# Row tiles in the third block of the first layer, sums of that block in A, and a new spread of the last copies

## The chip, the cores and the metric

One core of a Trainium2 chip runs the whole program in one launch. The metric is the device time of that launch in microseconds (us), the median over runs; less is better.

## The reference

An mLSTM attention over 2 x 8 heads and 768 steps gives 1536 tokens of 320 numbers. Two dense layers follow, each with a hidden width of 2048:

```python
def _moe_ref(x, w_in, w_out):          # the first layer
    h = x @ w_in
    g = where(h >= 1, h, where(h <= -1, 0.0, (h + 1) ** 2 / 4))
    return g @ w_out

def _moe2_ref(x, w_in, w_out):         # the second layer
    h = x @ w_in
    g = maximum(h, 0.0) + log1p(exp(-abs(h)))
    return g @ w_out
```

All is float32. Every product is made of two-part numbers, a high part and a rest, so that three matmuls (high x high, rest x high, high x rest) stand for one.

## The kernel before, in words

The tokens are cut into three blocks of 512 (`BLOCKS`, j = 0, 1, 2), the hidden width into 16 strips of 128 (f). PE takes, for every layer l and block j, an **up** step per strip (h = x times w_in, in PSUM) and a **down** step (g times w_out, summed over the strips in PSUM). Between them ACT and DVE make g: in the first layer `hinge` (ACT relu L834, ACT square L839, DVE min/max L843, which reads h again), in the second `softplus` (ACT L853, DVE L857, ACT L862, DVE L866); `split_g` then makes the high part gh (ACT L875) and the rest gl (DVE L879).

PSUM has eight banks here: one each for `ha` and `hb` (the h of even and odd strips), three in the tile D (`banks[1]`, key `ACC`) and three in the tile A (`banks[0]`, key `MIX`).

* The first layer works on the full 128-row array. `up` (L760 to L770) is 8 matmuls of 512 columns for a strip; `down1` (L885 to L902, matmuls L895 to L901) is 8 more, all of them into D. A block's sums leave D through `to_x` (L904 to L935): ACT and DVE copy them to the high part xh and the rest xl of the next layer's input, and the next block's sums wait for that.
* The second layer works on two **row tiles** of 64 rows, which take two matmuls at the same time. `slot` (L779 to L787) issues such a pair; every matmul of it has the line L783. `up2` (L800 to L827) does two strips f and f+1 in 8 slots and then 7 slots, 15 in all, since the last partial product needs only 64 rows; in the second half the row tiles swap banks. Two row tiles must not sum into one bank at the same time, so where a bank changes tiles, `hand_over` (L774 to L778) puts a no-op on POOL that waits for the matmuls that come first, and the matmul that comes next waits for POOL. `down2` (L941 on) does two strips in 24 slots of 320 columns, of which 3 are put between the halves of a later up pair.

What goes out in which order is set by `Plan` (L37 on), a list scheduler that knows each task's engine, cost, what it reads and writes, and for PE tasks a place `at`. Its result is a fixed order for each engine; the hardware waits only on semaphores. The second half of an up pair carries the key `("turn", ...)`, which the 3 down slots write, so that they come between. In the loop at the end, the first layer's `down1` comes `LAG = 3` strips after its `up`; the second layer's `down2` starts only with its own strips, so the first two up pairs of the second layer have nothing between their halves.

The last block's sums lie in A bank 2 and D banks 2, 0 and 1; four copies (L995 on DVE, L997 on ACT) bring them to SBUF and eight DMAs (L1008, on SP's, ACT's and POOL's queues) write them out.

Of the kernel before, what the change touches and what calls it, by code (L numbers as in the profile page):

```python
# [22 lines left out]
DM = H * D  # L23
# [186 lines left out]
def mlstm_moe_moe(ctx: ExitStack, tc: tile.TileContext, gates, late, qk, tok, ident, w1, w2, out):  # L210
    nc = tc.nc

    def pool(name, bufs, stack=ctx, **kw):
        return stack.enter_context(tc.tile_pool(name=name, bufs=bufs, **kw))

    BUFS = dict(raw=2, v=2, w=NF, u=3, gh=4, gl=4, xr=1, qx=3, tok=2, f=3, dec=2, sig=2, vi=2, ve=2,
                den=2, y=1, v2=10, e=3, o=4, x2=1, ha=1, hb=1, D=1, A=1)
    pools, tiles = {}, {}
# [34 lines left out]
    def vec(c):  # L253
        return 0.065 + c / 960
# [7 lines left out]
    def act(c):  # L262
        return 0.09 + c / 1075
# [494 lines left out]
    def up(l, j, f, at):  # L758
# [41 lines left out]
    def up2(j, f, at):  # L800
        n = BLOCKS[j][1]
        W, HP = ([(k, 1) + x for x in ((f,), (f + 1,))] if k == "w" else [(k, 1, j, f), (k, 1, j, f + 1)] for k in "wh")
        turn = {}

        def parts(i, r, s, e):
            w, hp = tiles[W[i]], tiles[HP[i]]
            ops = [(w[:, a + 128 * k:a + 128 * k + 128], xs) for k in range(2)
                   for a, xs in ((0, xh[j][:, k]), (0, xl[j][:, k]), (WC, xh[j][:, k]))]
            ops.append((w[:, 256:384], xh[j][:, 2]))
            if i == r:  # L810
                ops.append((w[:, WC + 256:WC + 384], tiles["x2", j] if r else xh[j][:, 2]))
# [8 lines left out]
        rd = [(W[i], k) for i in range(2) for k in range(2)] + xkeys(j) + [(("x2", j % 2),)]  # L820
        add("pe", 8 * (n / 2400 + 0.013), t, reads=rd, writes=[(x,) for x in HP],
            new=[(("ha", "hb")[i], HP[i]) for i in range(2)], at=at)

        def t():
            for k, pair in enumerate(zip(parts(1, 0, False, True), parts(0, 1, False, True))):
                slot(pair, None if k else turn.pop(0))
        add("pe", 7 * (n / 2400 + 0.013), t, reads=[*rd, (("turn", at - 40),)], writes=[(x,) for x in HP], at=at + 2)  # L827

    def hinge(j, f):
        n = BLOCKS[j][1]  # L830
        HP, U = ("h", 0, j, f), ("u", 0, j, f)
# [13 lines left out]
        add("dve", vec(n), t, reads=[(HP,)], writes=[(U,)])  # L845
        return U
# [23 lines left out]
    def split_g(l, j, f, G):  # L870
        n = BLOCKS[j][1]
        GH, GL = ("gh", l, j, f), ("gl", l, j, f)

        def t():
            nc.scalar.copy(new("gh", GH, [128, n], F32R), tiles[G])  # L875
        add("act", act(n), t, reads=[(G,)], writes=[(GH,)], new=[("gh", GH)])

        def t(e="dve"):
            (nc.gpsimd if e == "pool" else nc.vector).tensor_tensor(  # L879
                out=new("gl", GL, [128, n], F32R), in0=tiles[G], in1=tiles[GH].bitcast(F32), op=ALU.subtract)  # L880
        add("dve|pool" if (l, j) == (0, 0) else "dve", vec(n), t, port=True, reads=[(G,), (GH,)], writes=[(GL,)], new=[("gl", GL)])

    ACC, MIX = ("D",), ("A",)

    def down1(j, f, at):  # L885
# [16 lines left out]
        add("pe", 8 * (n / 2400 + 0.013), t, reads=[(W, 0), (W, 1), (GH,), (GL,)], writes=[(ACC, i) for i in [0, 1, 2, *("qps" if first else "")]], at=at)  # L902

    def to_x(j):  # L904
        n = BLOCKS[j][1]
        XR = ("xr", j)
        xk = xkeys(j)
        nh = [(("xh", j), i) for i in range(BLOCKS[j][0] // L, (BLOCKS[j][0] + n) // L)]
        nl = [(("xl", j), i) for i in range(BLOCKS[j][0] // L, (BLOCKS[j][0] + n) // L)]

        def t():
            nc.scalar.copy(new("xr", XR, [64, n]), banks[1][64:128, 2, 0:n])
        add("act", act(n), t, reads=[(ACC, 2)], writes=[(XR,)], new=[("xr", XR)])

        def t():
            nc.vector.tensor_tensor(out=tiles[XR], in0=banks[1][0:64, 2, 0:n], in1=tiles[XR], op=ALU.add)
        add("dve", vec(n), t, reads=[(ACC, 2)], writes=[(XR,)])
        for i in range(2):
            def t(i=i):
                nc.scalar.copy(xh[j][:, i], banks[1][:, i, 0:n])  # L920
            add("act", act(n), t, reads=[(ACC, i)] + (xk if i else []), writes=[(("xh", j, i),)] + ([] if i else xk))

            def t(i=i):
                nc.vector.tensor_tensor(  # L924
                    out=xl[j][:, i], in0=banks[1][:, i, 0:n], in1=xh[j][:, i].bitcast(F32), op=ALU.subtract)
            add("dve", vec(n), t, reads=[(ACC, i), (("xh", j, i),)], writes=[(("xl", j, i),)])
# [10 lines left out]
    nout = [0]  # L937

    handed = {}

    def down2(j, f, at):  # L941
# [37 lines left out]
        g = [k for k, _ in g]  # L979
        third_last = j == len(BLOCKS) - 1 and f == NF - 6  # L980
        cuts = [0, 18, 21, 24] if third_last else [0, 21, 24]
        for k0, k1, when in zip(cuts, cuts[1:], (3, 21, 22.5)):
            turn = [(("turn", at - 20),)] if when == 21 else []
            add("pe", (k1 - k0) * (DM / 2400 + 0.011), some(k0, k1), reads=g, writes=dk + turn, at=at + when)
        if e:
# [52 lines left out]
    def t():  # L1038
        phase.close()
        for name in ("v2", "e", "o", "x2"):  # L1040
            pools[name] = pool(name, BUFS[name])
# [4 lines left out]
    def t():  # L1046
        nc.scalar.preload_act_table_set("softplus")
    for g, (l, j, f) in enumerate(steps):
        if (l, j) == (1, 0):
            if f == 0:  # L1050
                add("act", 1.3, t, writes=TAB)
        if l == 0:
            up(l, j, f, 10 * g)
        elif f % 2 == 0:
            if f == 0:
                x2_copy(j)
            up2(j, f, 10 * g)
# [95 lines left out]
```

## Time and profile before

| | |
|---|---|
| median of 3 runs | 422.74 us (422.04 to 424.52) |
| the profiled execution: its own time | 427.52 us |
| its span, first to last instruction | 425.7 us |
| mean granted TensorE clock | 0.989 of full |
| PE busy | 406.3 us, 95% of the span |
| DVE busy | 288.2 us, 68% |
| ACT busy | 260.0 us, 61% |
| POOL busy | 38.3 us, 9% |

PE is the matmul stream, PEld the loading of its weights, which runs beside it. A matmul's duration in the profile is longer than the distance to the next one, since matmuls overlap in the array: the pace is read from the starts. The attention lies in the first 165 us, among the first layer's blocks 0 and 1; block 2 of the first layer runs from about 197 to 254 us, and from 258 us on there is the second layer alone.

### The profile page before, as it was taken

What the parts mean: (1) busy time and instruction counts of PE and PEld (TensorE: products, weight loads), DVE (VectorE), ACT (ScalarE), POOL (GpSimd) and SP (SyncE); (2) the same over time, 40 slices, a digit from 0 to 9 for tenths busy, and PEclk for the clock granted to TensorE, in tenths of its full rate; (3) what the DMA queues carried; (4) which work ended last, traced back from release to release, by engine and by line L of the source; (5) the groups of instructions that cost most, each with busy time, mean ns of one, the idle gap of its engine ahead of it and who ended that gap; (6) DMA issues with size and microseconds to landing.
All of it is one profiled execution on the core that took longest, in us unless ns stands there. A gap on an engine that the chain in (4) does not pass through costs nothing.

```text
span 425.7 us, 10004 instructions
## 1 busy us (share of the span) xinstructions
PE 406.3 (95%) x4211; PEld 346.7 (81%) x4211; DVE 288.2 (68%) x477; ACT 260.0 (61%) x451; POOL 38.3 (9%) x46
## 2 busy tenths in 40 slices
PE   6999889899999999999999999999999999999994
PEld 4556567688788888887888877989899999999993
DVE  4478799998987746656878668646474646564552
ACT  3224768887746459888888654636464545555451
POOL 3233222322411000000000000000000000000000
PEclk9998989999999999999999999999999999999998
DMA  8966767888672004554340000000010000010002
GB/s 300 324 225 226 228 191 241 289 287 255 199 226 74 2 2 137 203 201 140 110 147 16 0 2 0 2 2 2 2 48 17 2 2 2 24 41 2 1 2 63
DMA packets 13741, 45.05 MB, mean 106 GB/s; under 512 B 2320, under 2 KB 4048, under 8 KB 13696
## 3 DMA queue, kind: packets, MB, share of 16 engines
q1 hardware_dynamic: 12832, 43.22, 31.4%
q10 hardware_dynamic: 832, 1.11, 0.9%
q8 instruction: 33, 0.54, 0.5%
q14 instruction: 12, 0.10, 0.1%
q0 software_dynamic: 32, 0.08, 0.1%
HBM read 42.36 MB, written 2.05 MB: 104 GB/s over the span
## 4 chain that ended last, share of the span: by engine, by line
PE 84%; DVE 6%; ACT 5%; DMA 3%; issue 1%; POOLq 0%; SPq 0%; DVEq 0%
PE h L783 19%; PE h L769 16%; PE A L783 10%; PE D L783 10%; PE D L899 5%; PE D L901 5%; PE D L900 5%; PE D L895 3%; PE D L896 2%; PE fill L462 2%; DMA raw<-in_w_dram 2%; PE A L528 1%; DMA qx<-in_qk_dram 1%; PE A L507 1%; PE A L520 1%
## 5 line engine op out<-in xcount | busy, mean ns | idle before, releaser
L769 PE MATMUL h<-xh,w 128*128 128x512 f32 x288 | 90.5, 398 | 0.5 <-DVE u L843 0.4
L783 PE MATMUL h<-xh,w 64*128 64x512 f32 x504 | 87.4, 390 | 0.2
L857 DVE SCALAR_TENSOR_TENSOR e<-u,h 128x512 f32<-128x512 f32 x48 | 30.8, 684 | 61.0 <-ACT u L853 60.9
L783 PE MATMUL D<-w,gh 64*128 64x320 f32 x384 | 71.4, 306 | 0.7 <-DVE xl L924 0.7
L783 PE MATMUL A<-w,gh 64*128 64x320 f32 x384 | 70.6, 306 | 0.0
L879 DVE TENSOR_TENSOR gl<-u,gh 128x512 fp32r<-128x512 f32 x94 | 63.1, 693 | 10.1 <-ACT gh L875 8.0
L875 ACT CAST gh<-u 128x512 fp32r<-128x512 f32 x96 | 59.0, 621 | 14.1 <-DVE u L843 7.6
L769 PEld LDWEIGHTS h<-xh,w 128*128 128x128 f32 x288 | 54.5, 190 | 13.5 <-DVE w L749 0.9
L853 ACT ACTIVATE u<-h 128x512 f32<-128x512 f32 x48 | 26.1, 595 | 64.2 <-PE h L783 64.2
L783 PEld LDWEIGHTS h<-xh,w 64*128 64x128 f32 x504 | 55.3, 184 | 6.0 <-POOLq L775 1.1
L783 PEld LDWEIGHTS D<-w,gh 64*128 64x128 f32 x384 | 55.7, 184 | 1.8 <-DVE xl L924 1.2
L783 PEld LDWEIGHTS A<-w,gh 64*128 64x128 f32 x384 | 54.3, 184 | 0.7
L783 PE MATMUL D<-w,gl 64*128 64x320 f32 x192 | 50.4, 307 | 0.0
L783 PE MATMUL A<-w,gl 64*128 64x320 f32 x192 | 49.3, 307 | 0.0
L843 DVE SCALAR_TENSOR_TENSOR u<-u,h 128x512 f32<-128x512 f32 x48 | 32.7, 681 | 18.1 <-ACT u L839 16.9
L834 ACT ACTIVATE u<-h 128x512 f32<-128x512 f32 x48 | 28.6, 596 | 23.3 <-PE h L769 23.1
L783 PE MATMUL h<-xl,w 64*128 64x512 f32 x192 | 40.5, 392 | 0.0
L769 PE MATMUL h<-xl,w 128*128 128x512 f32 x96 | 38.0, 396 | 1.4 <-DVE xl L700 1.4
L899 PE MATMUL D<-gh,w 128*128 128x512 f32 x96 | 37.5, 390 | 0.0
L900 PE MATMUL D<-gh,w 128*128 128x512 f32 x96 | 37.4, 390 | 0.0
L901 PE MATMUL D<-gl,w 128*128 128x512 f32 x96 | 37.4, 389 | 0.0
L749 DVE TENSOR_TENSOR w<-v,w 128x704 fp32r<-128x704 f32 (+2 forms) x46 | 31.1, 705 | 4.1 <-ACT w L740 4.0
(127 smaller groups left out, 685.2 us busy)
## 6 DMA issues: line engine op xcount, KB each, us to landing
raw<-in_w_dram SPq DMA_DIRECT2D x32, 704.0 KB, 4.2
qx<-in_qk_dram SPq DMA_DIRECT2D x12, 640.0 KB, 7.0
tok<-in_tok_dram SPq DMA_DIRECT2D x12, 496.0 KB, 5.9
dec<-scr_d SPq DMA_DIRECT2D x16, 128.0 KB, 6.0
f<-scr_f SPq DMA_DIRECT2D x16, 128.0 KB, 6.1
out_dram<-o SPq DMA_DIRECT2D x20, 80.0 KB, 2.1
dec<-scr_d ACTq DMA_DIRECT2D x6, 128.0 KB, 6.9
out_dram<-o ACTq DMA_DIRECT2D x3, 80.0 KB, 2.2
```

Source lines behind the costliest of these rows:

```text
L749: eng.tensor_tensor(out=w[:, o:o + b - a], in0=v[:, a:b], in1=w[:, a:b].bitcast(F32), op=ALU.subtract)
L769: nc.tensor.matmul(hp, a, x, start=(i == 0), stop=(i == len(ops) - 1))
L783: mm = nc.tensor.matmul(o, a[half[r]], x[half[r]], start=s, stop=e)
L834: nc.scalar.activation(out=new("u", U, [128, n]), in_=tiles[HP], func=ACTF.Relu, scale=0.5, bias=0.5)
L843: nc.vector.scalar_tensor_tensor(out=tiles[U], in0=tiles[U], scalar=1.0, in1=tiles[HP], op0=ALU.min, op1=ALU.max)
L853: nc.scalar.activation(out=new("u", M, [128, n]), in_=tiles[HP], func=ACTF.Relu)
L857: nc.vector.scalar_tensor_tensor(out=new("e", E, [128, n]), in0=tiles[M], scalar=-2.0, in1=tiles[HP], op0=ALU.mult, op1=ALU.add)
L875: nc.scalar.copy(new("gh", GH, [128, n], F32R), tiles[G])
L879: (nc.gpsimd if e == "pool" else nc.vector).tensor_tensor(out=new("gl", GL, [128, n], F32R), in0=tiles[G], in1=tiles[GH].bitcast(F32), op= ...
L899: nc.tensor.matmul(d[i], hi[:, k], gh, start=s, stop=False)
L900: nc.tensor.matmul(d[i], lo[:, k], gh, start=False, stop=False)
L901: nc.tensor.matmul(d[i], hi[:, k], gl, start=False, stop=e)
```

## The change

1. The third block of the first layer, and the last four strips of the second block's down steps, go to row tiles. `up2` serves both layers. A new `pair1` does the down steps of two strips in 16 slots: a main part of 10 and a tail of 6.
2. The third block's sums go to A (`SUMS`). Of its up pairs, every second one (f = 2, 6, 10, 14) has its h in banks 0 and 1 of A (f = 2) or of D (the others) in place of `ha` and `hb`.
3. Down steps come in pairs, one pair of strips later (`pending`, `at = 10 * (g + 3)`), also across the border of the layers: the main part stands between the halves of an up pair, the tail behind the second half.
4. `to_x` takes the banks in the order 1, 0 and, for the third block, copies bank 1 on DVE and bank 0 on ACT.
5. In the second layer the sums of the three blocks have fixed banks (`softs`); the last block's are A 2, D 2, A 0, D 0. The first down pair is cut at slot 6, the last one at slot 18.
6. Buffers: `gl` 3 and a new `gx` 1 instead of `gl` 4; `y` 2 instead of 1; `v2` 9 instead of 10. The `x2` copies, one per block on row tiles, are four instead of three.

```diff
-    def up2(j, f, at):
+    ACC, MIX = ("D",), ("A",)
+    SUMS = [(ACC, 1), (ACC, 1), (MIX, 0)]
+    ROWS = [(0, 2), (1, 0), (1, 1), (1, 2)]
...
+    def up2(l, j, f, at):
         n = BLOCKS[j][1]
+        lo = (WC + 64, WC)[l]
...
+        mixed = l == 0 and f % 4 == 2
+        hk = [((ACC, MIX)[f == 2], i) for i in range(2)] if mixed else [(x,) for x in HP]
...
             for i in range(2):
-                new(("ha", "hb")[i], HP[i], [128, n])
+                if mixed:
+                    tiles[HP[i]] = banks[f > 2][:, i, 0:n]
+                else:
+                    new(("ha", "hb")[i], HP[i], [128, n])
...
-        add("pe", 7 * (n / 2400 + 0.013), t, reads=[*rd, (("turn", at - 40),)], writes=[(x,) for x in HP], at=at + 2)
+        add("pe", 7 * (n / 2400 + 0.013), t, reads=[*rd, (("mid", at),)], writes=hk, at=at + 2)
...
+    def pair1(j, f, at):
...
+        def jobs(order, begins, ends):
+            done = []
+            for b in order:
+                d = banks[SUMS[j][1]][:, b, 0:n]
+                ops = []
+                for i in range(2):
+                    w, gh, gl = tiles[W[i]], tiles[GH[i]], tiles[GL[i]]
+                    hi, lo, r = w[:, 384:640], w[:, WC + 64 + 384:2 * WC], w[:, 640:768]
+                    k = slice(128 * b, 128 * b + 128)
+                    ops += [(r, gh), (r, gl)] if b == 2 else [(hi[:, k], gh), (lo[:, k], gh), (hi[:, k], gl)]
...
+        def main():
+            for k, pair in enumerate(zip(jobs((1, 2), (1,), (2,)), jobs((2, 0), (2, 0), ()))):
+                last = slot(pair, handed.pop((j, f, k), None))
+                if k == 3:
+                    handed[j, f, 6] = hand_over(last)
+            handed[j, f, "tail"] = hand_over(last)
+
+        def tail():
+            for k, pair in enumerate(zip(jobs((0,), (), (0,)), jobs((1,), (), (1,)))):
+                last = slot(pair, None if k else handed.pop((j, f, "tail")))
+            if not e:
+                handed[j, f + 2, 0] = hand_over(last)
...
+        when = {(1, NF - 4): (-1, 1), (2, NF - 2): (-15, 1)}.get((j, f), (1, 3))
...
-        for i in range(2):
-            def t(i=i):
-                nc.scalar.copy(xh[j][:, i], banks[1][:, i, 0:n])
+        for k, i in enumerate((1, 0)):
+            def t(i=i, k=k):
+                (nc.scalar.copy if k or j < 2 else nc.vector.tensor_copy)(xh[j][:, i], banks[SUMS[j][1]][:, i, 0:n])
...
-        cuts = [0, 18, 21, 24] if third_last else [0, 21, 24]
+        cuts = {(0, 0): [0, 6, 21, 24], (2, NF - 6): [0, 18, 21, 24], (2, NF - 2): [0, 18, 24]}.get((j, f), [0, 21, 24])
...
+    softs = [
+        [(ACC, 0), (ACC, 1), (ACC, 2), (MIX, 2)],
+        [(MIX, 0), (ACC, 0), (MIX, 1), (ACC, 1)],
+        [(MIX, 2), (ACC, 2), (MIX, 0), (ACC, 0)]]
...
+    def downs(n):
+        while n:
+            n -= 1
+            l, j, f, at = pending.pop(0)
+            (pair1, down2)[l](j, f, at)
+            if l == 0 and f == NF - 2:
+                to_x(j)
...
-        if l == 0:
+        if (l, j) not in ROWS:
             up(l, j, f, 10 * g)
...
-        if l == 0:
-            down1(j, f, 10 * (g + LAG) + 6)
+        if l == 0 and f < (NF, NF - 4, 0)[j]:
+            down1(j, f, 10 * (g + LAG) + (12 if (j, f) == (1, NF - 5) else 6))
...
         elif f % 2:
-            down2(j, f - 1, 10 * (g + 1))
+            pending.append((l, j, f - 1, 10 * (g + 3)))
+            downs(len(pending) - 1)
```

In the instruction orders below a name such as `u_2_3_2553` holds block, strip and a buffer number, and `h_0_1` is an h. DVE at the start of the third block, before:

```order
L843 SCALAR_TENSOR_TENSOR u_2_2_2472<-u_2_2_2472,h_2_2_2445 128x512
L924 TENSOR_TENSOR xl_135<-D,xh_132 128x512
L916 TENSOR_TENSOR xr_2489<-D,xr_2489 64x512
L924 TENSOR_TENSOR xl_135<-D,xh_132 128x512
L879 TENSOR_TENSOR gl_2_2_2509<-u_2_2_2472,gh_2_2_2506 128x512
L843 SCALAR_TENSOR_TENSOR u_2_3_2503<-u_2_3_2503,h_2_3_2476 128x512
```

And in the change:

```order
L970 TENSOR_TENSOR xr_2533<-D,xr_2533 64x512
L860 SCALAR_TENSOR_TENSOR u_2_2_2548<-u_2_2_2548,A 128x512
L860 SCALAR_TENSOR_TENSOR u_2_3_2553<-u_2_3_2553,A 128x512
L978 TENSOR_TENSOR xl_135<-D,xh_132 128x512 x2
L898 TENSOR_TENSOR gl_2_2_2608<-u_2_2_2548,gh_2_2_2603 128x512
L898 TENSOR_TENSOR gl_2_3_2611<-u_2_3_2553,gh_2_3_2606 128x512
```

The h of strips 2 and 3 now lies in A, DVE reads both behind one step of the second block's `to_x`, and the xl steps come behind them.

PE in the first up pair of the second layer, the last slot of the first half and the first slots of the second half, before:

```order
L783 MATMUL h_0_0_2899<-xh_131,w_0_2537 128x512
L783 MATMUL h_0_1_2900<-id_h,w_1_2554 128x512
L783 MATMUL h_0_1_2900<-xh_131,w_1_2554 128x512
L783 MATMUL h_0_0_2899<-xh_131,w_0_2537 128x512
L783 MATMUL h_0_1_2900<-xl_134,w_1_2554 128x512
```

And in the change, from the first row behind the first half on:

```order
L784 MATMUL A<-gh_2_12_3088,w_12_1354 128x512 x3
L784 MATMUL A<-gl_2_12_3106,w_12_1354 128x512 x2
L784 MATMUL A<-gh_2_13_3104,w_13_1482 128x512 x2
L784 MATMUL A<-gl_2_13_3108,w_13_1482 128x512
L784 MATMUL A<-gh_2_13_3104,w_13_1482 128x512
L784 MATMUL A<-gh_2_12_3088,w_12_1354 128x512
L784 MATMUL A<-gl_2_13_3108,w_13_1482 128x512
L784 MATMUL A<-gh_2_12_3088,w_12_1354 128x512 x2
L784 MATMUL A<-gl_2_12_3106,w_12_1354 128x512 x2
L784 MATMUL A<-gh_2_13_3104,w_13_1482 128x512 x3
L784 MATMUL A<-gl_2_13_3108,w_13_1482 128x512 x2
L784 MATMUL h_0_1_3130<-xh_131,w_1_2667 128x512
```

Ten slots of the first layer's down pair of strips 12 and 13 now stand between the halves.

ACT at the end of the program, before:

```order
L875 CAST gh_2_15_5424<-u_2_15_5405 128x512
L997 COPY o_2_5480<-D 128x320
L997 COPY o_3_5484<-D 128x320
L1008 DMA out_dram<-o_2_5480 64x320
L1008 DMA out_dram<-o_2_5480 64x320
L1008 DMA out_dram<-o_3_5484 64x320
```

And in the change:

```order
L894 CAST gh_2_15_5728<-u_2_15_5709 128x512
L1044 COPY o_2_5784<-A 128x320
L1055 DMA out_dram<-o_2_5784 64x320
L1044 COPY o_3_5792<-D 128x320
L1055 DMA out_dram<-o_2_5784 64x320
L1055 DMA out_dram<-o_3_5792 64x320
```

Result 2 now comes from A, which closes six slots before the end, and one DMA stands ahead of the second copy. On DVE the two last rows are the copies of results 0 and 1 in both, the first from A and the second from D; before, the second stands behind both copies of ACT, in the change ACT's second copy stands behind it.

## Rows read from the trace of the kernel before

**Rows 1.** The page, section 1: busy time, share of the span, instructions.

```profile
PE 406.3 (95%) x4211; PEld 346.7 (81%) x4211; DVE 288.2 (68%) x477; ACT 260.0 (61%) x451; POOL 38.3 (9%) x46
```

**Rows 2.** Busy time by stage: stretch, PE, PEld, DVE, ACT, POOL, PEclk, DMA share, GB/s.

```profile
200.00:246.00 46.00, 45.60 (x202) 37.46 (x200) 35.71 (x53) 38.60 (x62) 0.00 (x0) 1.00 0.19 64
```

**Rows 3.** Timeline of PE, full array: start, length, instruction (128 matmuls between these starts).

```profile
165.74 0.39 PE L895 MATMUL D<-gh,w 128*128 128x512 f32 x1
...
194.75 0.39 PE L895 MATMUL D<-gh,w 128*128 128x512 f32 x1
```

**Rows 4.** Timeline of PE, row tiles: one up and down pair of layer two.

```profile
269.17 0.39 PE L783 MATMUL h<-xh,w 64*128 64x512 f32 x2
...
271.01 0.30 PE L783 MATMUL D<-w,gh 64*128 64x320 f32 x1
...
273.06 0.45 PE L783 MATMUL A<-w,gh 64*128 64x320 f32 x4
...
276.13 0.39 PE L783 MATMUL h<-xh,w 64*128 64x512 f32 x2
```

**Rows 5.** Timeline of PE from 199 to 265 us, places where it waits or switches.

```profile
199.51 0.84 PE L769 MATMUL h<-xh,w 128*128 128x512 f32 x3
200.76 0.47 PE L895 MATMUL D<-gh,w 128*128 128x512 f32 x1 [0.40 <-DVE xl L924]
...
245.95 0.39 PE L901 MATMUL D<-gl,w 128*128 128x512 f32 x1
246.26 0.50 PE L783 MATMUL h<-xh,w 64*128 64x512 f32 x2
246.60 0.40 PE L783 MATMUL h<-xl,w 64*128 64x512 f32 x2
...
255.91 0.39 PE L783 MATMUL h<-id_h,w 64*128 64x512 f32 x1
256.41 0.50 PE L783 MATMUL h<-xh,w 64*128 64x512 f32 x2
...
263.94 0.41 PE L783 MATMUL D<-w,gh 64*128 64x320 f32 x1 [0.74 <-DVE xl L924]
...
264.49 0.39 PE L783 MATMUL h<-xh,w 64*128 64x512 f32 x2
```

**Rows 6.** Timeline: an up pair's last matmuls, then ACT and DVE behind them.

```profile
272.61 0.62 PE L783 MATMUL h<-xh,w 64*128 64x512 f32 x4
...
273.32 1.09 ACT L853 ACTIVATE u<-h 128x512 f32<-128x512 f32 x2 [3.00 <-PE h L783]
...
273.95 1.28 DVE L857 SCALAR_TENSOR_TENSOR e<-u,h 128x512 f32<-128x512 f32 x2 [2.90 <-ACT u L853]
```

**Rows 7.** Groups by line from 150 us on: count, busy us, mean ns, idle before.

```profile
L783 PEld LDWEIGHTS D<-w,gh 64*128 64x128 f32 x384 | 55.7, 184 | 1.8 <-DVE xl L924 1.2
...
L924 DVE TENSOR_TENSOR xl<-D,xh 128x512 fp32r<-128x512 f32 x4 | 2.7, 685 | 1.7 <-PE A L783 1.1 <-ACT xr L912 0.6
L920 ACT CAST xh<-D 128x512 fp32r<-128x512 f32 x4 | 2.4, 588 | 1.7 <-DVE xl L924 0.8 <-DVE xr L916 0.7
```

**Rows 8.** Timeline of the end: last matmuls, copies and DMA issues.

```profile
419.69 0.31 PE L783 MATMUL D<-w,gl 64*128 64x320 f32 x2
420.04 0.75 ACT L997 COPY o<-D 128x320 f32<-128x320 f32 x2 [3.87 <-PE D L783]
420.50 1.86 ACTq L1008 DMA_DIRECT2D out_dram<-o  x3
420.83 0.49 DVE L995 COPY o<-D 128x320 f32<-128x320 f32 x1 [1.18 <-ACT o L997]
421.94 0.70 POOL L1008 DMA_DIRECT2D out_dram<-o  x1 [278.57 <-DMA out_dram<-o]
```

**Rows 9.** DMA issues from 415 us on: KB each, median us to landing.

```profile
out_dram<-o ACTq DMA_DIRECT2D x3, 80.0 KB, 2.2
out_dram<-o POOLq DMA_DIRECT2D x1, 80.0 KB, 2.3
```

More of the change, by code (lines that the diff above doesn't have):

```diff
@@ L819, in t @@
             turn[0] = hand_over(last)
-        rd = [(W[i], k) for i in range(2) for k in range(2)] + xkeys(j) + [(("x2", j % 2),)]
-        add("pe", 8 * (n / 2400 + 0.013), t, reads=rd, writes=[(x,) for x in HP],
-            new=[(("ha", "hb")[i], HP[i]) for i in range(2)], at=at)
+        rd = [(W[i], k) for i in range(2) for k in range(2)] + xkeys(j) + [(X2,)]
+        add("pe", 8 * (n / 2400 + 0.013), t, reads=rd, writes=hk,
+            new=[] if mixed else [(("ha", "hb")[i], HP[i]) for i in range(2)], at=at)
         def t():
@@ L872, in split_g @@
         GH, GL = ("gh", l, j, f), ("gl", l, j, f)
+        fourth = f % 4 == 3 and ((l, j) in ROWS or (l, j, f) == (0, 1, NF - 1))
+        tag = "gx" if fourth else "gl"
         def t():
@@ L879, in t @@
             (nc.gpsimd if e == "pool" else nc.vector).tensor_tensor(
-                out=new("gl", GL, [128, n], F32R), in0=tiles[G], in1=tiles[GH].bitcast(F32), op=ALU.subtract)
-        add("dve|pool" if (l, j) == (0, 0) else "dve", vec(n), t, port=True, reads=[(G,), (GH,)], writes=[(GL,)], new=[("gl", GL)])
-    ACC, MIX = ("D",), ("A",)
+                out=new(tag, GL, [128, n], F32R), in0=tiles[G], in1=tiles[GH].bitcast(F32), op=ALU.subtract)
+        add("dve|pool" if (l, j) == (0, 0) else "dve", vec(n), t, port=True, reads=[(G,), (GH,)] + ([*ATT] if fourth else []), writes=[(GL,)], new=[(tag, GL)])
     def down1(j, f, at):
@@ L902, in down1 @@
         add("pe", 8 * (n / 2400 + 0.013), t, reads=[(W, 0), (W, 1), (GH,), (GL,)], writes=[(ACC, i) for i in [0, 1, 2, *("qps" if first else "")]], at=at)
+    def pair1(j, f, at):
+        n = BLOCKS[j][1]
+        W, GH, GL = ([(k, 0) + ((f + i,) if k == "w" else (j, f + i)) for i in range(2)] for k in ("w", "gh", "gl"))
+        s, e = f == 0, f == NF - 2
+        def jobs(order, begins, ends):
[3 more added lines that the diff above has]
+                ops = []
+                for i in range(2):
+                    w, gh, gl = tiles[W[i]], tiles[GH[i]], tiles[GL[i]]
+                    hi, lo, r = w[:, 384:640], w[:, WC + 64 + 384:2 * WC], w[:, 640:768]
+                    k = slice(128 * b, 128 * b + 128)
+                    ops += [(r, gh), (r, gl)] if b == 2 else [(hi[:, k], gh), (lo[:, k], gh), (hi[:, k], gl)]
+                done += [(d, a, x, s and b in begins and q == 0, e and b in ends and q == len(ops) - 1) for q, (a, x) in enumerate(ops)]
+            return done
+        def main():
[9 more added lines that the diff above has]
+                handed[j, f + 2, 0] = hand_over(last)
+        g = [k for i in range(2) for k in ((W[i], 0), (W[i], 1), (GH[i],), (GL[i],))]
+        acc = [(SUMS[j][0], i) for i in range(3)]
+        when = {(1, NF - 4): (-1, 1), (2, NF - 2): (-15, 1)}.get((j, f), (1, 3))
+        mid = [[(("mid", at),)] if x == 1 else [] for x in when]
+        add("pe", 10 * (n / 2400 + 0.013), main, reads=g, writes=acc + mid[0], at=at + when[0])
+        add("pe", 6 * (n / 2400 + 0.013), tail, reads=g, writes=acc[:2] + mid[1], at=at + when[1])
     def to_x(j):
@@ L979, in down2 @@
         g = [k for k, _ in g]
[L980 to L984 removed]
+        cuts = {(0, 0): [0, 6, 21, 24], (2, NF - 6): [0, 18, 21, 24], (2, NF - 2): [0, 18, 24]}.get((j, f), [0, 21, 24])
+        for k0, k1, when in zip(cuts, cuts[1:], (-17, -16, 1) if (j, f) == (0, 0) else (-17, 1, 2.5)):
+            mid = [(("mid", at),)] if when == 1 else []
+            x = [(("xl", 2, i),) for i in range(2)] if (j, f, k0) == (0, 0, 6) else []
+            to = {(0, 6): dk[:3], (18, 24): dk[1::2]}.get((k0, k1), dk)
+            add("pe", (k1 - k0) * (DM / 2400 + 0.011), some(k0, k1), reads=g + x, writes=to + mid, at=at + when)
         if e:
@@ L1039, in t @@
         phase.close()
[L1040 removed]
+        for name in ("v2", "e", "o", "x2", "gx"):
             pools[name] = pool(name, BUFS[name])
```

63 lines of the change are left out of this document (32 added, 31 removed).

## The prediction, on record before the run

> **What bounds the kernel now.** The page's first section shows PE busy for 95% of the span and every other engine for 68% or less [rows 1]. A mean says little about a stage, so the next view is the busy time by stage. In the third block of the first layer (200 to 246 us) PE is busy for 45.60 of 46 us; the granted clock is 1.00, the upper of its two levels, 2.4 GHz [rows 2]. So here time goes away only if PE has fewer slots, or loses less between them. The third view is PE's timeline, read from start to start.
>
> The pace of the full array is 29.01 us for 128 matmuls, 0.2266 us each [rows 3]. On row tiles, 8 slots of 512 columns take 1.84 us, 0.230 each, and 21 slots of 320 columns take 3.07 us, 0.1462 each; a whole pair of the second layer takes 6.96 us [rows 4], which is 15 x 0.230 + 24 x 0.1462.
>
> What is lost between slots follows from one stretch, 199.51 to 264.49 us, 64.98 us [rows 5]. By the code, 3 matmuls of one up step and 200 + 16 later ones are on the full array (219 x 0.2266 = 49.63), 15 + 15 + 8 are slots of 512 columns (8.74) and 21 + 3 of 320 (3.51): 61.88 us. **3.10 us are lost**, and the rows show where. The third block's first sums wait until D is free of the second block: due at 199.96 + 0.23 = 200.19, begun at 200.76. A switch from the array to row tiles: due at 246.18, begun at 246.26, and the next slot only 0.34 later, so 0.19 in all; the program switches forth, back and forth again around 250 and 254 us. The first two up pairs of the second layer have a hand-over through POOL with nothing between their halves; in the second pair the half begins 0.50 after the last slot's start (255.91 to 256.41), where 0.23 would be its pace. And the second layer's sums in D wait for the third block's xl, 0.74 us before 263.94. After each stop the first slot is some 0.1 longer, as after the switch. The stop at 200 us doesn't lower the clock [rows 2].
>
> **The change, part by part.**
>
> *Slots.* Removed are 16 strips x 16 matmuls and 4 x 8 down matmuls, 288 x 0.2266 = 65.27 us. Added are 8 pairs of 15 + 16 slots and 2 pairs of 16, 280 x 0.230 = 64.40 us. Gain 0.87 us. No row shows a down slot of 512 columns on row tiles. I take the up slot, which has the same two loads and the same columns; the ends are the full array's pace (280 x 0.2266, gain 1.8) and, above, what the rivals say. The row tiles' slot is 3.4 ns dearer than the array's matmul. The Trainium skill, TensorE: Matmul & The Clock Gate, section "Measured speedup vs the span model", gives a pack of n tiles the time of one matmul and some 4 ns for each further tile; that would be 280 x 0.2306 and a gain of 0.70. The rows give 3.4 ns, and they decide.
>
> *Stops between slots.* Gone are the two switches around 250 us, both bare hand-overs (ten slots now stand there, by the second order), and the long waits at both block borders in their old form. Of the 3.10 us, four items stay or come:
> - One switch to row tiles, now in the second block: 0.19 [rows 5].
> - The third block's first sums go to A, where strips 2 and 3 have their h. They start 8 slots behind the second block's tail, 9 x 0.230 = 2.07 after that tail's last start, and wait for DVE to have read both. From a last matmul's start to ACT are 0.48 us (272.84 to 273.32), and two DVE steps take 1.28, so they follow each other at 0.60 and the last ends after 0.68 [rows 6]. DVE does one xr step and the two min/max steps (first order): 0.48 + 0.60 + 0.60 + 0.68 + 0.05 = 2.41. Late by 0.34, with the slow first slot 0.45. ACT's two relu and two squares, 0.50 apart (two take 1.09 [rows 6]), are in time: 0.48 + 3 x 0.50 + 0.60 + 0.05 + 0.68 + 0.05 = 3.36 of the 15 x 0.230 = 3.45 from the up pair's last start. Bounds: 0, and the 0.65 that the same border costs now.
> - Strips 14 and 15's main part stands directly behind the tail of 12 and 13, so one hand-over is bare: 0.27 as now [rows 5], with the first slot 0.38.
> - The second layer's first sums take six slots in D and then need A. From the last tail slot there are 8 x 0.230 + 6 x 0.1462 = 2.72 us; ACT's copy 0.59, DVE's copy and two xl steps (0.60 + 0.60 + 0.69) and three hops come to 0.48 + 0.59 + 0.05 + 1.89 + 0.05 = 3.06 [rows 6, 7]. Late by 0.34, with the first slot 0.45. Bounds: 0, and the same wait now, 0.74 and a slow first slot.
>
> Together 1.47 instead of 3.10: gain 1.63, between 1.0 and 2.5 if the two waits are both as long as now or both nought.
>
> *Turn-taking inside a pair.* The main part hands a bank over between its slots 3 and 6, three slots or 0.69 us. A bare hand-over takes 0.50 from start to start [rows 5], so I cost it at nothing; its cover is the two slots between, and without them it would be 0.27 each, ten times. Otherwise there are 7 slots from a main part to its tail and 8 from a tail to the next main part.
>
> *ACT and DVE.* ACT has 38.60 us of work in 46 us of this stage [rows 2], 6.1 per pair of strips where PE now takes 7.25 and then 31 x 0.230 = 7.13. A pair's gh and gl are wanted 31 + 14 slots after its up, and h has four banks instead of two. The split of g thus lies beside PE; nothing added. One x2 copy more (0.6 on ACT) and one buffer fewer for v2 lie there too. SP's and POOL's other work keeps its order.
>
> *The end.* Now PE ends at 420.00, ACT copies twice, DVE's copy of result 1 comes behind them and ends at 421.32, POOL's DMA begins at 421.94 and lands 2.3 later, 4.24 us after PE's end [rows 8, 9]. In the change DVE copies result 1 first, ending 0.53 after PE; POOL's DMA, again 0.62 later, would land at +3.45. ACT's second copy then ends at about +1.0, and its last DMA begins one issue (1.86 / 3 = 0.62) later and lands 2.2 after that, at +3.8. Gain 0.45; bounds 0, if something else holds the end, and 0.8, POOL's own part.
>
> **Sum.** 0.87 + 1.63 + 0.45 = 2.95 us. The profiled execution took 427.52 us (span 425.7 and 1.8 around it) and would take 424.6; the median of the timed runs is 422.74, 1.1% less, and the same 2.95 us off it gives **419.8 us**. All lies at one clock level, so no other scale is needed. With each term at its ends the gain lies between 0.9 + 1.0 + 0 = 1.9 and 1.8 + 2.5 + 0.8 = 5.1; all upper ends at once are not likely, and I take 418.7 to 420.8.
>
> **The rivals.**
>
> 1. *The stops move and don't go.* Each of the two waits at the borders keeps its present length, or the hand-over inside the main parts is late by some 0.1 us ten times over. For it: the two chains are mine, step by step, and a DVE step that slips in front adds 0.60 at once. Against it: a cover of 0.69 against 0.50 measured, and chains shorter than now. Then the stops cost 3.10 as now and only slots and end count: 422.74 - 0.87 - 0.45 = 421.4.
>
> 2. *Loads show in the new down slots, slower than before.* A down slot of 512 columns on row tiles might cost more than an up slot: it changes both weights and the moving tile between gh and gl, and 160 of the 280 slots are such. At 0.230 + 2.95 / 160 = 0.248 the gain is used up; at 0.27 the time is 419.8 + 160 x 0.04 = 426.2, and with a whole load of 0.184 [rows 7] in each 419.8 + 29.4 = 449. Against it: the second layer's down slots of 320 columns do the same and run at 0.1462, the column share of the up slot. The Trainium skill, TensorE: Matmul & The Clock Gate, section "The mechanism", lets a weight load run beside a matmul only if it is for other rows of the array, by which every slot would show its load. The up slots at 0.230, with two loads of 0.184 each, contradict it here, so the chance stays small.
>
> 3. *The change doesn't give PE anything*, since ACT takes over the third block: from 7.13 us of ACT work per pair on PE waits, and at 7.13 + 2.95 / 8 = 7.50 nothing is left, 422.7. It has 6.1.
>
> **How the numbers follow.** Forecast 0.69, rival 1 0.20, rival 2 0.07, rival 3 0.04. A measurement of this kernel can tell about 0.5%, 2.1 us, from no change, so faster means below 420.6. Of the forecast 0.65 lie there and 0.04 above it; of rival 1, by scatter, 0.03; rival 2 is slower by more than the bound with 0.05, the rest of it and rival 3 are within. Faster 0.68, same 0.27, slower 0.05. The range runs from the forecast's lower end to rival 1 with some scatter of the runs, 418.7 to 422.0, and leaves out rivals 2 and 3 and the forecast's outer tails.
>
> **What would show it.** Right: from the third block on, all of PE's matmuls on row tiles at 0.230 with 7.1 us per pair; one switch; bare hand-over once; PE waiting for DVE once before the first sums in A and once before the second layer's first sums, 0.3 to 0.5 us each; the last DMA landing 0.4 us closer to PE's end. Wrong: a pair of the third block above 7.25 us, a wait of PE for gh or gl in it, or a stop of a microsecond at either border.

## The result and the profile after

The changed kernel takes 420.45 us in the median of 20 runs (417.96 to 424.79), against 424.16 us (421.89 to 427.59, 20 runs): ratio 0.991, 95% interval 0.9885 to 0.9937, so 3.7 us less (2.7 to 4.9). The forecast was 419.8 us and a gain of 2.95.

A single run scatters by 2 us and more either way, and the profiles show where: the attention's last transposes begin anywhere from 155.6 to 161.8 us, in kernels whose order up to there is all but the same. What comes behind them hardly scatters: it is 254.38 to 254.45 us in four profiles with the same order there (the change twice, experiments 2 and 5). The kernel before has one profile only. So the kernels are compared by two stretches of their profiles: **part**, from the start of the down matmul behind the last transposes to the start of PE's last slot, and **rest**, from there to the span's end (page, to 0.1 us). Some expectations below count from the row of the transposes (160.57 in the change), 0.24 us earlier.

| kernel | part, us | rest, us | ratio to the kernel before (runs) |
|---|---|---|---|
| before | 419.69 - 162.00 = 257.69 | 6.0 | |
| the change | 415.20 - 160.81 = 254.39 | 5.8 | 0.991 (20) |
| the change again | 254.45 | 5.8 | 0.989, 0.986 to 0.993 (9) |

The part became 3.30 us shorter, the rest 0.2, together 3.5. The medians differ by 3.7, and 3.5 lies within their interval.

The page's first section and the stage of [rows 2] in the change:

```profile
PE 398.9 (95%) x4483; PEld 348.5 (83%) x4483; DVE 289.1 (69%) x481; ACT 256.2 (61%) x448; POOL 38.5 (9%) x46
```

```profile
200.00:246.00 46.00, 46.00 (x408) 37.81 (x406) 36.84 (x56) 34.93 (x58) 0.00 (x0) 1.00 0.24 80
204.60:239.73 35.13, 35.13 (x313) 28.89 (x310) 28.96 (x45) 29.99 (x49) 0.00 (x0) 1.00 0.31 104
```

PE is busy all 46 us, and the clock is at its upper level (1.00) as before. The second stretch is five pairs of strips, in which ACT has 29.99 us of work and DVE 28.96: 6.0 and 5.8 per pair. PE's timeline, places that answer to [rows 5]:

```profile
182.46 0.39 PE L918 MATMUL D<-gl,w 128*128 128x512 f32 x1
182.78 0.73 PE L784 MATMUL D<-gh,w 64*128 64x512 f32 x3
183.12 0.62 PE L784 MATMUL D<-gl,w 64*128 64x512 f32 x2
...
198.13 0.84 PE L784 MATMUL h<-xh,w 64*128 64x512 f32 x5
199.22 0.73 PE L784 MATMUL A<-gh,w 64*128 64x512 f32 x3 [0.22 <-DVE u L860]
199.56 0.62 PE L784 MATMUL A<-gl,w 64*128 64x512 f32 x2
...
204.60 0.39 PE L784 MATMUL D<-xh,w 64*128 64x512 f32 x2
...
206.19 0.39 PE L784 MATMUL D<-id_h,w 64*128 64x512 f32 x1
...
239.73 0.39 PE L784 MATMUL h<-xh,w 64*128 64x512 f32 x2
...
246.53 0.39 PE L784 MATMUL A<-gl,w 64*128 64x512 f32 x2
247.12 0.70 PE L784 MATMUL A<-gh,w 64*128 64x512 f32 x3 [0.20 <-POOLq L776]
247.46 0.59 PE L784 MATMUL A<-gl,w 64*128 64x512 f32 x2
...
255.15 0.31 PE L784 MATMUL D<-w,gh 64*128 64x320 f32 x1
255.48 0.41 PE L784 MATMUL A<-w,gh 64*128 64x320 f32 x1
255.74 0.30 PE L784 MATMUL A<-w,gh 64*128 64x320 f32 x1
```

DVE in the change ahead of the sums that begin at 199.22, the xr step and then the two min/max steps:

```profile
197.30 0.68 DVE L970 TENSOR_TENSOR xr<-D,xr 64x512 f32<-64x512 f32 x1 [1.62 <-PE D L784]
197.90 1.27 DVE L860 SCALAR_TENSOR_TENSOR u<-u,A 128x512 f32<-128x512 f32 x2
```

**Slots.** From 204.60 to 239.73 are five pairs of 15 + 16 slots: 35.13 / 155 = 0.2266 us each, up and down alike. That is the array's pace [rows 3], not the 0.230 of [rows 4].

**Stops.** At the four places the rows take more than their slots would at full pace: 0.66 - 0.453 = 0.21 (two slots, 182.46 to 183.12), 1.43 - 0.907 = 0.52 (four slots, 198.13 to 199.56), 0.93 - 0.453 = 0.48 (two slots, 246.53 to 247.46) and 0.59 - 0.292 = 0.30 (two slots of 320 columns at 0.1462, 255.15 to 255.74; what PE waits for there is DVE's xl). The 0.48 is some 0.03 too much, since the row of 247.46 is the second matmul of its slot. Together they are 1.5; the forecast had 1.47.

The end in the change, which answers to [rows 8]:

```profile
414.67 0.43 ACT L1044 COPY o<-A 128x320 f32<-128x320 f32 x1 [2.99 <-PE A L784]
415.13 0.49 DVE L1042 COPY o<-A 128x320 f32<-128x320 f32 x1 [2.73 <-ACT o L1044]
415.20 0.31 PE L784 MATMUL D<-w,gl 64*128 64x320 f32 x2
415.55 0.49 DVE L1042 COPY o<-D 128x320 f32<-128x320 f32 x1
415.65 2.52 SPq L1055 DMA_DIRECT2D out_dram<-o  x4
416.07 0.43 ACT L1044 COPY o<-D 128x320 f32<-128x320 f32 x1 [0.98 <-DVE o L1042]
416.08 1.15 ACTq L1055 DMA_DIRECT2D out_dram<-o  x2
416.70 0.70 POOL L1055 DMA_DIRECT2D out_dram<-o  x1 [274.52 <-ACT o L1044]
```

POOL's DMA now begins at 416.70, 1.50 behind PE's last slot, where it was 2.25 (421.94 - 419.69). But SP's queue issues four DMAs from 415.65 on, 2.52 us in all, so the last of them begins at about 417.6.

### The profile page after: what moved, and what is told of

It reads as the page before. It is cut to its first block, busy times and chain, and to the rows that moved or that the text cites. A ratio compares the mean times of both kernels' runs of the same rounds, so it can differ in the third digit from the quotient of the medians.

```text
span 421.0 us, 10618 instructions
## 1 busy us (share of the span) xinstructions
PE 398.9 (95%) x4483; PEld 348.5 (83%) x4483; DVE 289.1 (69%) x481; ACT 256.2 (61%) x448; POOL 38.5 (9%) x46
## 4 chain that ended last, share of the span: by engine, by line
PE 79%; DVE 10%; DMA 4%; ACT 3%; issue 2%; SPq 1%; POOLq 0%; DVEq 0%
PE h L784 22%; PE A L784 16%; PE D L784 16%; PE h L769 9%; DVE v L728 2%; PE fill L462 2%; PE D L916 2%; PE D L918 2%; PE D L917 2%; DMA raw<-in_w_dram 2%; DVE u L860 2%; DMA f<-scr_f 2%; DVE w L749 1%; DMA qx<-in_qk_dram 1%; PE D L912 1%
## 5 line engine op out<-in xcount | busy, mean ns | idle before, releaser
L784 PE MATMUL h<-xh,w 64*128 64x512 f32 x588 | 102.8, 388 | 0.0
L769 PE MATMUL h<-xh,w 128*128 128x512 f32 x192 | 60.2, 399 | 1.2 <-DVE w L749 0.7
L769 PEld LDWEIGHTS h<-xh,w 128*128 128x128 f32 x192 | 35.8, 188 | 10.4 <-DVE w L749 2.0
L784 PE MATMUL A<-w,gh 64*128 64x320 f32 x320 | 44.3, 305 | 0.0
L784 PEld LDWEIGHTS A<-w,gh 64*128 64x128 f32 x320 | 35.8, 184 | 0.3 <-DVE xl L978 0.3
L728 DVE SCALAR_TENSOR_TENSOR v<-raw,v 128x704 int32<-128x704 int32 x32 | 30.0, 939 | 6.4 <-ACT v L721 6.3
L879 ACT ACTIVATE e<-e 128x512 f32<-128x512 f32 x48 | 29.4, 632 | 6.1 <-DVE e L874 6.1
L883 DVE TENSOR_TENSOR u<-u,e 128x512 f32<-128x512 f32 x48 | 31.0, 689 | 2.6 <-ACT e L879 0.5
L784 PE MATMUL A<-w,gl 64*128 64x320 f32 x160 | 32.2, 309 | 0.0
L717 ACT ACTIVATE v<-raw 128x704 f32<-128x704 int8 x32 | 27.1, 847 | 8.0 <-DMA raw<-in_w_dram 7.7
```

The source lines that it names most:

```text
L717: nc.scalar.activation(out=v.bitcast(F32), in_=top, func=ACTF.Prelu, bias=-56.0, alpha=2.0 ** -40)
L728: nc.vector.scalar_tensor_tensor(out=tiles[V], in0=mid, scalar=5, in1=tiles[V], op0=ALU.logical_shift_right, op1=ALU.bitwise_or)
L769: nc.tensor.matmul(hp, a, x, start=(i == 0), stop=(i == len(ops) - 1))
L784: mm = nc.tensor.matmul(o, a[half[r]], x[half[r]], start=s, stop=e)
L879: nc.scalar.activation(out=tiles[E], in_=tiles[E], func=ACTF.Softplus)
L883: nc.vector.tensor_tensor(out=tiles[M], in0=tiles[M], in1=tiles[E], op=ALU.add)
```

## The experiments

All are edits of the changed kernel. Experiments 1 and 3 to 7 have one profiled run each, so they are read from the part and the rest; 2 and 8 to 10 have six runs each.

**1. What PE waits for at the border of the blocks.** In `to_x` for the second block, DVE's sum xr waits for the min/max of strip 3 (the call of `to_x` moves behind that strip for it, not shown).

```diff
-        add("dve", vec(n), t, reads=[(SUMS[j][0], 2)], writes=[(XR,)])
+        add("dve", vec(n), t, reads=[(SUMS[j][0], 2)] + [(("u", 0, 2, 3),)] * (j == 1), writes=[(XR,)])
...
```

> Edit: the DVE step that adds the two halves of the second block's rest (xr) comes behind the min/max steps of strips 2 and 3 of the third block instead of ahead of them. Theory: PE's wait before the third block's first sums in A (0.42 us, to 199.22) is DVE's chain, and xr is 0.6 us of it; without it the second min/max ends at about 198.7 where PE is due at 198.81, so the wait, the slow first slot (0.11) and the slow slots behind it go: 0.5 us less from the attention's last transposes to the span's end (260.44 now, 259.9 then). Rival: ACT's squares or the up pair itself hold the first sums; then the wait stays at 0.3 us or more and the part stays within 0.1 of 260.4.

The part is 412.45 - 158.49 = 253.96, 0.43 less than in the change. PE and DVE at the border:

```profile
195.16 1.28 DVE L860 SCALAR_TENSOR_TENSOR u<-u,A 128x512 f32<-128x512 f32 x2 [1.00 <-ACT u L856]
196.26 0.39 PE L784 MATMUL h<-id_h,w 64*128 64x512 f32 x1
196.50 0.73 PE L784 MATMUL A<-gh,w 64*128 64x512 f32 x3
196.84 0.62 PE L784 MATMUL A<-gl,w 64*128 64x512 f32 x2
```

DVE's two min/max steps now run from 195.16 for 1.28 us, to 196.44, and PE's first sums in A start on time. The theory holds: xr stood in the way. But the second distance is still 0.34: this slot, behind a wait that ends just in time, is as slow as the one behind the stop in the change (199.22 to 199.56). So 0.43 went and not 0.5.

**2. The second y buffer.** `y=2` becomes `y=1`.

> Edit: one buffer for y instead of two; the order of every engine is the same. In the two profiles the attention's last transposes begin 1.18 us earlier in the change (160.57 against 161.75). Theory: that is scatter of the stage that waits for DMAs, and the buffer is worth nothing; time within 0.7 us of the change's 420.45, and 260.4 us from the last transposes to the span's end. Rival: the second y buffer lets the attention run ahead and is worth about 1 us; then the median is 421.5 or more.

The median of 6 runs is 419.42 us, 0.989 of the kernel before (0.985 to 0.994); the part is 254.38, and the transposes begin at 156.53. The median lies 1.0 below the change's, where the theory allowed 0.7, but single runs scatter by more, and the rival wanted 421.5. So the buffer shows no gain, and the earlier transposes in the first profile of the change were scatter (155.62 in the change again).

**3. What a long slot costs behind shorter ones.**

```diff
+                if k < 3:
+                    last = slot(pair, None if k else handed.pop((j, f, "tail")))
+                    continue
+                for c in (slice(0, 192), slice(192, 512)):
+                    last = slot([(d[:, c], a, x[:, c], b, y and c.start > 0) for d, a, x, b, y in pair])
```

> Edit: in the ten tails on row tiles the last three slots of 512 columns are each cut into one of 192 and one of 320 columns; nothing else. Theory: a row tile's slot has the array's pace of 0.2267 us, and the 0.230 that the forecast used is the price of the first six long slots behind a run of shorter ones (0.230, 0.236, 0.228, 0.232, 0.231, some 0.024 us together). Then each tail costs 3 x 0.0133 for the three more slots and 0.024 behind it: 10 x 0.064 = 0.64, and the part from the last transposes to the span's end is 261.1 instead of 260.44; the up slots behind a tail show the row of numbers above. Rival: 0.230 belongs to the second layer's own slots (its weights, or the place of its tiles); then only the three more slots count, 0.40, 260.85, and the up slots behind a tail stay at 0.2267.

The part is 255.53, 1.14 more than in the change. A tail and the up slots behind it:

```profile
203.05 0.68 PE L784 MATMUL A<-gh,w 64*128 64x192 f32 x8
...
203.83 0.39 PE L784 MATMUL D<-xh,w 64*128 64x512 f32 x2
...
204.98 0.85 PE L784 MATMUL D<-xh,w 64*128 64x512 f32 x5
205.45 0.39 PE L784 MATMUL D<-id_h,w 64*128 64x512 f32 x1
205.67 0.61 PE L784 MATMUL A<-gh,w 64*128 64x512 f32 x3
```

The seven up slots from 203.83 to 205.45 take 1.62 us, 0.23 each; the same seven in the change, 204.60 to 206.19, take 1.59. Behind them the old pace is back (205.45 to 205.67). So 0.230 is no property of the second layer or of row tiles: it follows a run of shorter matmuls and is over after some seven slots. The size was off elsewhere: the six short slots take 0.78 (203.05 to 203.83) and not 0.72, a price that neither theory had. Against three long slots (0.68) that is 0.10 more, and with the 0.03 behind them 1.3 for ten tails, near the 1.14 measured.

The kernel before shows the same, on row tiles behind slots of 320 columns (the row here lies between the first two of [rows 4]) and on the full array behind the transposes of 128:

```profile
270.33 0.84 PE L783 MATMUL h<-xh,w 64*128 64x512 f32 x5
```

```profile
162.31 0.39 PE L896 MATMUL D<-gl,w 128*128 128x512 f32 x1
...
163.70 0.39 PE L901 MATMUL D<-gl,w 128*128 128x512 f32 x1
```

Five slots of 0.232 (269.17 to 270.33) and three of 0.227 (to 271.01) on the row tiles; on the array six matmuls take 1.39, some 0.23 each.

**4. How much cover the turn-taking needs.**

```diff
+            one = jobs((1, 2), (1,), (2,))
+            one = one[:5] + one[6:] + one[5:6]
...
-                    handed[j, f, 6] = hand_over(last)
+                    handed[j, f, 5] = hand_over(last)
```

> Edit: in the main part of a down pair the row tile that takes over bank 2 does so at slot 5 instead of 6 (one slot of its first bank is moved behind), so one slot instead of two lies under the hand-over through POOL. Theory (the forecast's rival 1 in its own place): the hand-over needs 0.50 to 0.59 us from start to start, as where it is bare; two slots between leave 0.68 and hide it, one leaves 0.453 and doesn't: a stop of 0.05 to 0.14 and 0.1 of slow slots behind it in ten main parts, 1.5 to 2.5 us, 262 to 263 from the last transposes to the span's end. Rival: POOL answers fast enough while PE's queue runs ahead; then the part stays at 260.4.

The part is 256.38, 1.99 more than in the change, 0.2 for each of ten main parts:

```profile
212.62 0.39 PE L784 MATMUL A<-gl,w 64*128 64x512 f32 x1
212.85 0.80 PE L784 MATMUL A<-gh,w 64*128 64x512 f32 x4
213.49 0.39 PE L784 MATMUL A<-gl,w 64*128 64x512 f32 x2
```

Slot 3 starts at 212.62, and the two slots from 212.85 to 213.49 take 0.64 in place of 0.453. So POOL's hand-over takes longer than the two slots from 3 to 5, and the three from slot 3 to slot 6 of the change hide it. The second half of rival 1 (the main parts' hand-over is late) is excluded for the change, if only by one slot.

**5. What holds the end.**

```diff
-                    q = (("sp", "sp"), ("sp", "pool"), ("act", "act"), ("act", "sp"))[i][b] if j == len(BLOCKS) - 1 else "sp"
+                    q = (("sp", "sp"), ("sp", "pool"), ("act", "act"), ("act", "act"))[i][b] if j == len(BLOCKS) - 1 else "sp"
```

> Edit: the last of SP's four DMAs of the last block's results goes to ACT's queue, which issues three now; all else stays. In the change PE's last slot starts at 415.20 and the span ends 5.81 us later. Theory: SP's queue holds the end: its four issues take 2.5 us from 415.65 on and the fourth begins at 417.6, behind ACT's last (about 416.7) and POOL's (416.70). Without it SP's last begins at about 416.9 and ACT's fourth at about 417.2: 0.3 to 0.4 us less, the span ends 5.4 to 5.5 us behind PE's last slot. Rival: POOL's DMA, or what comes behind all DMAs, holds the end; then 5.8 stays.

The part is 254.39 as in the change, the rest 421.0 - 415.42 = 5.6, 0.2 less (0.3 was the theory's lower end). All four kernels with this edit (experiments 5, 8, 9 and 10) have 5.6; the other eight profiles of the change and its edits have 5.7 to 6.0.

```profile
415.87 1.86 SPq L1055 DMA_DIRECT2D out_dram<-o  x3
416.30 1.81 ACTq L1055 DMA_DIRECT2D out_dram<-o  x3
416.93 0.70 POOL L1055 DMA_DIRECT2D out_dram<-o  x1 [274.52 <-ACT o L1044]
```

SP's queue did hold the end, and POOL's DMA did not: it begins 1.5 behind PE's last slot in both. ACT's queue is now the last to issue, until 418.1. The Trainium skill, DMA: Bandwidth & Descriptors, section "Rules for kernel authors", says that spreading DMAs over the issuing engines saves only the time of issue. The rows show that saving, 1.86 us for three in place of 2.52 for four; what it does to the bandwidth no run here tells.

**6. The bare hand-over at the end of the third block.** Strips 14 and 15 stand directly behind the tail of 12 and 13; here their two row tiles change places, so that each goes on with a bank it had.

```diff
+        turned = (j, f) == (2, NF - 2)
+
+        def tiles_of(a, b):
+            return enumerate(zip(b, a) if turned else zip(a, b))
...
-            if not e:
+            if f + 2 < NF - 2 + 2 * (j == 1) and not e:
```

> Edit: in the last down pair of the third block (strips 14 and 15), which stands directly behind the tail of 12 and 13, the two row tiles change places, so each begins with a bank that it had itself, and no hand-over through POOL stands there. Theory: the stop in the change (0.36 us from 246.53 on, and 0.08 and some slow slots behind it) is that hand-over alone: 0.45 us less from the last transposes to PE's last slot (254.41 now, 253.96 then), and the wait for DVE's xl at 255.15 keeps its 0.19. Rival: the stop hides another wait (gh or gl of strips 14 and 15), or the time comes back as a longer wait for xl; then less than 0.2 us.

The part is 253.84, 0.55 less than in the change. PE at the place (tail to 242.62, main part from 242.84):

```profile
242.62 0.39 PE L784 MATMUL A<-gl,w 64*128 64x512 f32 x2
242.84 0.39 PE L784 MATMUL A<-gh,w 64*128 64x512 f32 x2
243.07 0.39 PE L784 MATMUL A<-gl,w 64*128 64x512 f32 x1
```

No stop and no slow slot: the theory holds, and the wait for xl did not grow (250.75 to 251.05, 0.30 from start to start, where it was 0.33).

**7. Row tiles earlier.** The second block's strips 12 to 15 go up, and 8 to 15 down, on row tiles.

```diff
-ROWS = [(0, 2), (1, 0), (1, 1), (1, 2)]
+ROWS = [(0, 1), (0, 2), (1, 0), (1, 1), (1, 2)]
+
+    def tiled(l, j, f):
+        return (l, j) in ROWS and ((l, j) != (0, 1) or f >= NF - 4)
...
```

> Edit: the row tiles begin earlier: also the up steps of the second block's strips 12 to 15 and its down steps from strip 8 on. By the slot count each up pair saves one slot of 0.2267, two pairs 0.45 us; the down steps save nothing (16 slots for 16 matmuls). Theory: nothing else changes, 254.41 from the last transposes to PE's last slot becomes 253.96. Rival: the pair-wise down steps are wanted earlier behind their min/max than the single ones, or the attention's last steps keep A from the up pair; then a new wait eats the 0.45.

The part is 254.13, 0.26 less than in the change instead of 0.45: partly the rival. PE comes to the border sooner and waits there longer: 196.97 to 197.68 is 0.71, where the change has 0.64 (198.13 to 199.22 without two slots). And a slot at 193.89 is 0.1 slow. The two make 0.17 of the 0.19 that is missing.

**8. Four of them together (1, 5, 6, 7).**

> All four edits at once: xr behind the min/max steps (measured alone: 0.42 us less up to PE's last slot), the row tiles of strips 14 and 15 changed round (0.45 expected), SP's last DMA on ACT (0.35), row tiles from the second block's strip 12 on (0.45). Theory: they lie in different places and add up to 1.6 to 1.7 us: 252.8 to 253.1 from the last transposes to PE's last slot and 5.5 behind it, time about 418.8, 0.987 of the kernel before. Rival: they share waits at the borders of the blocks (the earlier row tiles move the border at which xr was late), and less than 1.2 us is left.

The part is 253.76, only 0.63 less than in the change, and the rest 5.6; the time is 418.35 us, 0.987 of the kernel before (0.982 to 0.992). The rival holds. ACT and PE at the border:

```profile
193.54 0.83 ACT L717 ACTIVATE v<-raw 128x704 f32<-128x704 int8 x1
194.40 0.79 ACT L721 ACTIVATE v<-v 128x704 int32<-128x704 f32 x1
195.21 1.09 ACT L856 ACTIVATE u<-A 128x512 f32<-128x512 f32 x2
```

```profile
197.40 0.39 PE L784 MATMUL h<-x,w 64*128 64x512 f32 x1
198.19 0.73 PE L784 MATMUL A<-gh,w 64*128 64x512 f32 x3 [0.41 <-DVE u L865]
```

The scheduler put two steps of a weight ahead of the relu of strips 2 and 3, on the chain that PE waits for. Experiment 9 tests that.

**9. The same with the weight moved behind the border, and gl late in the last pair.** The second layer's weights from strip 8 on wait for the min/max of strip 3; in the last down pair the first 12 slots are in another order.

```diff
+                if end:
+                    turns[:12] = [turns[k] for k in (0, 1, 3, 4, 6, 7, 2, 9, 5, 10, 8, 11)]
...
```

> The four edits together gave 0.62 us up to PE's last slot instead of 1.3: in front of the third block's first sums ACT took two steps of a weight (v of the second layer's strip 8) ahead of the relu of strips 2 and 3, so these began 0.35 us late and PE waited 0.64. Two edits more: the weights of the second layer from strip 8 on wait for the min/max of strip 3, and in the last down pair of all the products with gl come as late as the banks' turns allow. Theory: the 0.64 at the border goes (0.42 as in the run of xr alone, and the rest), the two waits for gl in the last pair shrink from 0.27 and the slow slots behind them by 0.3 together: 252.8 from the last transposes to PE's last slot (254.42 in the change), 5.55 behind it; about 1.9 us less than the change, 418.5, 0.986 to 0.987 of the kernel before. Rival: PE, now earlier everywhere, waits at the border for another step of the same chain (the up pair in A ends no earlier against it); then 253.2 or more.

The part is 252.93 (252.8 in theory) and the rest 5.6. The median is 417.24 us (415.98 to 418.29, 6 runs), 0.983 of the kernel before (0.980 to 0.987): faster than the kernel before and than the change, which took 420.09 beside it. PE at the border:

```profile
195.44 0.39 PE L784 MATMUL h<-x,w 64*128 64x512 f32 x1
195.66 0.73 PE L784 MATMUL A<-gh,w 64*128 64x512 f32 x3
```

From the last up matmul's start to the first sum 0.22 us pass, where it was 0.79 in experiment 8 (197.40 to 198.19). So the two weight steps were what PE waited for.

**10. The same without 7 and the weight's edit.**

> As the run before, without the earlier row tiles in the second block and without the edit of the weights: xr late, strips 14 and 15 changed round, SP's last DMA on ACT, gl late in the last pair. Theory: the parts add up where the borders stay as they were: 0.42 + 0.53 + 0.3 = 1.25 up to PE's last slot (253.15), 5.55 behind it; 1.5 us less than the change, about 418.9. Rival: gl of the last strip holds PE's end whatever the order; then 253.4 and no less.

The part is 253.27, 1.12 less than in the change (1.25 expected); the time is 418.71 us, 0.988 (0.984 to 0.991). The parts nearly add up where no border moves. And gl's place did shorten the end: the first twelve slots of the last pair take 2.01 (408.82 to 410.83) where the change takes 2.28 (411.30 to 413.58). The third kernel of that comparison, the change itself, for which stood:

> The changed kernel itself, beside the two below on one chip. All theories: 254.4 us from the last transposes to PE's last slot and 5.8 behind it, as in its first profile; 0.991 of the kernel before, with 0.3% either way.

gave 254.45 and 0.989, as in the table.

## Why the prediction was right, and where not

The sign, the main mechanism (PE bound, time goes only by slots and stops) and the range were right; two terms were mis-sized with opposite signs (the slots too low by 0.9, the end too high by 0.25), and the base was low.

* **Slots: forecast 0.87, came 1.8.** The failed step is "I take the up slot", 0.230 us. That is the mean of 8 slots behind shorter ones [rows 4]: five at 0.232 and three at 0.227. The third block's slots all have 512 columns, so only the second value applied, and 8 slots fewer at 0.2266 are 1.81 us, the other end that was named. Experiment 3 shows the cause. The Trainium skill, TensorE: Matmul & The Clock Gate, section "Measured speedup vs the span model", adds some 4 ns to a pack for each further tile. In the pace of this stream they do not show: 155 slots of two tiles take 0.2266 us each, as single matmuls do.
* **Stops: forecast 1.63, came 1.49** (3.30 - 1.81, the rest of the part's gain). The four items came at 0.21, 0.52, 0.48 and 0.30 where 0.19, 0.45, 0.38 and 0.45 stood: right in cause and in sum, though errors of 0.07 to 0.15 either way cancel in that sum. The 0.14 that is missing is the difference of two small things. With the 38 up slots at 0.2266 too, the kernel before lost 3.23 in that stretch and not 3.10. And 3.23 - 1.49 = 1.74 is left in the change, 0.27 more than the forecast's 1.47, mostly because the slots behind each stop are slow by some 0.004 each and no item has them. Experiment 1 confirms DVE's chain with xr in it, and experiment 6 the bare hand-over as the whole of its item. That hand-over took 0.59 from start to start and not 0.50, and the wait for xl was 0.15 shorter.
* **Turn-taking at nothing:** right. Experiment 4 prices it at 0.2 us per main part with one slot less of cover.
* **ACT and DVE hidden:** right, 6.0 us of ACT and 5.8 of DVE per pair against PE's 35.13 / 5 = 7.03.
* **End: forecast 0.45, came 0.2** (0.1 to 0.3 by the scatter of the rest in experiment 5; the kernel before has one profile). The step compared POOL's and ACT's last DMAs and left out SP's queue, whose row stood among those of the end of the kernel before:

```profile
419.68 2.96 SPq L1008 DMA_DIRECT2D out_dram<-o  x4
```

  Its last issue, at about 419.68 + 0.75 x 2.96 = 421.9, stood beside POOL's 421.94, and the DMA view from 421.9 us on gives it the longer landing (POOL's has 2.3 [rows 9]):

```profile
out_dram<-o SPq DMA_DIRECT2D x1, 80.0 KB, 2.7
```

  POOL's part shrank by 0.75, as forecast, but SP's is what remained (experiment 5).
* **The base.** The three runs shown had a median of 422.74; 20 runs gave 424.16, 1.4 us more. The gain was forecast 0.6 to 0.8 too small, so the two errors nearly cancel, and that 420.45 stands only 0.65 above the forecast is luck. The bound for "faster", 420.6, came from the same low base: that the change is faster rests on the ratio's interval, 0.9885 to 0.9937, and not on the 0.15 between 420.45 and that bound.

Of the rivals, 1 (the stops only move) falls with the stops' 1.49 and with experiment 4; 2 (loads show in the down slots) with 0.2266 for up and down slots alike, though each has two loads of 0.184 as in [rows 7] (its argument from the 0.1462 was a little off: the column share of 0.230 is 0.144); 3 (ACT bound) with its 6.0 per pair. Of the signs, one switch, one bare hand-over and one wait for DVE at each border came as said; "0.230" was wrong, and the rest behind PE's last slot shrank by 0.2 and not 0.4.

## What to carry to other kernels

Read a pace from the inner slots of a long run of one shape: the first five to ten behind a stop, a switch or shorter matmuls can be dearer, and a mean over eight of them mis-sizes a long stretch by a per cent or two. When work is moved to an earlier place, look at what the scheduler now puts in front of the first step of the chain that PE waits for; here one small step of DVE or two of ACT ahead of it cost 0.4 to 0.6 us, about what the two slots of experiment 7 were to save. At the end of a program count every queue's issues one behind another, not only the queue that the change touches.

## What was not expected of the hardware

Long matmuls (512 columns) behind shorter matmuls take some 0.231 instead of 0.2266 us for five to seven, on the full array as on row tiles; behind a switch or a hand-over on row tiles it is five to some ten (in the change ten slots from 199.80 to 202.10 take 2.30). It is not so behind every stop: in the kernel before, behind the one that ends at 200.76 [rows 5], only the first distance is long, 0.31, and the next is 0.22 again (201.07 to 201.29). The slot behind a wait that ends just in time takes 0.34, as behind a real stop (experiment 1, 196.50 to 196.84). Slots of 192 and 320 columns in turn take 0.78 us for six, where three of 512 take 0.68 (experiment 3). Why the first slots are slow was not tried and stays open.
